# Linear attention times a SwiGLU gate on one core: a seventh stored key operand, and the last two stores on SyncE

## The chip, the core and the metric

The kernel runs on one core of one Trainium2 chip. It uses that core's engines: TensorE (PE, matrix products; its weight loads are listed as PEld), VectorE (DVE), ScalarE (ACT), GpSimd (POOL) and SyncE (SP). SyncE only issues DMAs here. GpSimd issues DMAs and does some elementwise work. Sixteen DMA engines move the data of both. The metric is device time in microseconds (us) of one execution; less is better.

## The reference

x has 2048 rows of 1024 columns. The result is x + s * g, with

```python
def _A_ref(x, wqkv, wo):                 # 32 heads of width 32
    q, k, v = ...                        # x @ wqkv, by head
    phi = lambda t: jnp.where(t > 0, t + 1, jnp.exp(t)) + 1e-6
    pq, pk = phi(q), phi(k)
    kv = jnp.einsum("bhsd,bhse->bhde", pk, v)
    z = jnp.einsum("bhsd->bhd", pk)
    num = jnp.einsum("bhqd,bhde->bhqe", pq, kv)
    den = jnp.einsum("bhqd,bhd->bhq", pq, z)[..., None] + 1e-6
    return (num / den) @ wo              # heads side by side again

def _B_ref(x, w1, w3, w2):
    return (_silu(x @ w1) * (x @ w3)) @ w2

xn = _layernorm(x)
s = _A_ref(xn, A_wqkv, A_wo)
g = _silu(_B_ref(xn, B_w1, B_w3, B_w2))
return x + s * g
```

All inputs and the result are float32.

## The kernel before

**Products.** Every large product is made of blocks by a scheme with seven products in place of eight; the sums of blocks that it needs are operands of their own (names such as A11, S1 to S4 on the left, B11, T1 to T4 on the right). Each operand is split into a high and a low part (`split`, L91: a cast on ScalarE, L95, and a subtraction on VectorE, L96), and each block product is three matmuls (`mm3`, L100).

**Stages.** The rows are taken in two halves (h = 0, 1). In each half the keys and queries are made, and later the gate and up products of the SwiGLU layer. Between the queries and the gate of the second half stand the row products: since kv = pk^T v and v = xn w_v, the kernel first forms pk^T xn (over all 2048 rows) and multiplies by w_v afterwards. Then follow the attention's output products and the second layer (w2), whose last pass finishes the result.

**Key sums (`key_rows`, L519).** For each half and each of four pairs, four blocks of keys pass through phi, are turned by TensorE (L513) and written out by GpSimd as operands of the row products (`keep_keys`, L516): Y00, Y01, Y10, and the sums R5, R2 and R4. Six operands of 256 KB are stored for each of the eight pairs. y00 and r2 are tiles from `small`, which has six buffers (tag "c") shared with the products' results c22, c21, c12 and others.

**Row products (`row_products`, L558).** Seven products (`ROWS`, L625) go over four steps each: h = 0, 1 and t = 0, 2, so 28 steps. A step loads two row tiles of the left operand (x_d, L572) and two of the right one (y_d, L570) into one tile `xy<i>_<h><t>` of tag "raw", which has two buffers; splits them into tiles of tag "b", which has eight, four to a step; and multiplies each of the two row tiles into four banks. A step is 24 matmuls. The load for a step is written two steps ahead. The seventh product needs R2 - Y00: its steps load Y00 into a further tile `yy` (tag "job", four buffers) and subtract it on GpSimd (L583) before the split.

```python
            if less:
                other = job_tile([P, 2, C], f"yy{i}_{h}{t}")
                rows(other, less)
        ...
            if other is not None:
                nc.gpsimd.tensor_sub(out=raw[:, 2:], in0=raw[:, 2:], in1=other)
```

**Work between.** During the row products, small pieces of other work run between the steps: the denominators (L857 on TensorE, one for each of sixteen loads `pqd` into "job" tiles, then `r` and its store r_d). After them comes the division of the queries (`divide`, L872): each piece `qd<m>_<k>` is a "job" tile filled by two loads from r_d (L882) and two from pq_d (L884) on SyncE. In the last steps the weights of the first gate product (`wg`, L326) are loaded into a "raw" tile.

**Order.** The program is written in one stream. A scheduler places each instruction in its engine's queue by a modelled time and by when a buffer comes free; each queue is then worked through in order, and an instruction that has to wait holds all behind it. SyncE's queue is one: a load that waits for its tile holds every later load.

**The end (`finish`, L1191).** Each of the four blocks (t, n) of a 256-row tile m is finished by a silu on ScalarE (L1198), a product with s (`ss`, loaded on SyncE) and an addition of x (`xs`) on VectorE (L1199, L1201), and a store on GpSimd (L1202). The last tile is m = 7; its blocks end in the order (1,1), (0,0), (1,0), (0,1).

Of the kernel before, what the change touches and what calls it, by code (L numbers as in the profile page):

```python
# [16 lines left out]
P = 128  # L17
C = 512
# [4 lines left out]
def tile_linear_attention_times_swiglu(  # L23
# [58 lines left out]
    s_d = [dram.tile([P, D], F32, name=f"s_d{t}") for t in range(S // P)]  # L82
    AOPS = ["A11", "S2", "S3", "S1", "A12", "A22", "S4"]
    XS = ["A11", "A12", "S1", "S3", "A22", "S2", "S4"]
    YS = ["Y00", "Y01", "Y10", "R5", "R2", "R4"]
    x_d = [dram.tile([P, TH // 2, len(XS), C], F32, name=f"x_d{h}") for h in range(NH)]
    y_d = [dram.tile([P, TH // 2, len(YS), ND // 2, P], F32, name=f"y_d{h}") for h in range(NH)]
    g_d = [dram.tile([P, ND // 2, C], F32, name=f"g_d{n}") for n in range(4)]
# [27 lines left out]
    def small(name):  # L116
        return pc.tile([P, C], F32, tag="c", name=name)
# [401 lines left out]
    def key_rows(h, pair):  # L519

        rows = {}

        def use(n, c, src):
            j = 2 * pair + n
            pk = signed(f"pk{h}_{j}_{c}")
            z = st.tile([P, 1], F32, tag="z", name="z")
            phi(src, pk, z)
            nc.vector.scalar_tensor_tensor(zacc[:, j:j + 1], z, C * 1e-6, zacc[:, j:j + 1],
                                           op0=ALU.add, op1=ALU.add)
            later.append([3, lambda: turn(n, c, pk)])  # L530

        def turn(n, c, pk):
            V = nc.vector
            p_ = turned(pk, f"k{h}_{pair}_{n}{c}")
            if (c, n) == (0, 0):
                y00 = small(f"y00_{h}_{pair}")
                nc.scalar.activation(y00, p_, AF.Identity, bias=eps)  # L537
                keep_keys(h, pair, "Y00", y00)
            elif (c, n) == (1, 1):
                rows["y01"] = job_tile([P, 2, C], f"y01_{h}_{pair}")  # L540
                nc.scalar.copy(out=rows["y01"][:, 1], in_=p_)
            elif (c, n) == (1, 0):
                y10, r5 = (rows.setdefault("y10", job_tile([P, 2, C], f"y10_{h}_{pair}"))[:, e] for e in range(2))
                nc.scalar.activation(y10, p_, AF.Identity, bias=eps)
                V.tensor_sub(out=r5, in0=rows["y01"][:, 1], in1=p_)
                keep_keys(h, pair, "Y10", y10)
                keep_keys(h, pair, "R5", r5)
            else:
                (y01, r4), r5, r2 = (rows["y01"][:, e] for e in range(2)), rows["y10"][:, 1], small(f"r2_{h}_{pair}")
                nc.scalar.activation(y01, p_, AF.Identity, bias=eps)  # L550
                V.scalar_tensor_tensor(r4, p_, 2e-6, r4, op0=ALU.add, op1=ALU.add)
                V.scalar_tensor_tensor(r2, p_, 1e-6, r5, op0=ALU.add, op1=ALU.add)
                for n_, t in (("Y01", y01), ("R4", r4), ("R2", r2)):
                    keep_keys(h, pair, n_, t)

        return use

    def row_products():  # L558

        nonlocal stages  # L560
        ks = [(h, t) for h in range(NH) for t in range(0, TH // 2, 2)]
        steps = [(i, *k) for i in range(len(ROWS)) for k in ks]

        def load(i, h, t):
            x_, y_, less = ROWS[i]
            raw = praw.tile([P, 4, C], F32, tag="raw", name=f"xy{i}_{h}{t}")

            def rows(dst, n):
                src = y_d[h][:, t:t + 2, YS.index(n)].rearrange("p t j d -> p t (j d)")
                nc.sync.dma_start(out=dst, in_=src)  # L570

            nc.sync.dma_start(out=raw[:, :2], in_=x_d[h][:, t:t + 2, XS.index(x_)])  # L572
            rows(raw[:, 2:], y_)
            other = None
            if less:
                other = job_tile([P, 2, C], f"yy{i}_{h}{t}")
                rows(other, less)
            return raw, other

        def ready(i, h, t):  # L580
            raw, other = data[i, h, t]
            if other is not None:
                nc.gpsimd.tensor_sub(out=raw[:, 2:], in0=raw[:, 2:], in1=other)  # L583
            out = []
            for e in range(2):
                pair = []
                for n in range(2):
                    o = pb.tile([P, 2, C], FR, tag="b", name=f"xy{n}_{i}_{h}{t + e}")
                    split(o, raw[:, 2 * n + e])
                    pair.append(o)  # L590
                out.append(pair)
            return out

        data = {s: load(*s) for s in steps[:2]}
        split_ = {steps[0]: ready(*steps[0])}
        u, v, b = {}, {}, {}
        M = range(ND // 2)
        for at, s in enumerate(steps):
            i, h, t = s
            if at + 2 < len(steps):  # L600
                data[steps[at + 2]] = load(*steps[at + 2])
            if at + 1 < len(steps):
                split_[steps[at + 1]] = ready(*steps[at + 1])
            if at + 2 == len(steps):
                ops["g1_0_"].ask()
                stages = in_turn(groups[after_rows:])
            if at + 1 == len(steps):
                for _ in range(3):
                    next(stages)
            begins, ends = s[1:] == ks[0], s[1:] == ks[-1]  # L610
            onto = i in (1, 5)
            if begins and not onto:
                b = {m: bank(f"g{i}_{m}") for m in M}
            for e, (x_, y_) in enumerate(split_.pop(s)):
                for m in M:
                    c = slice(m * P, (m + 1) * P)
                    last = mm3(b[m], (x_[:, 0, c], x_[:, 1, c]), (y_[:, 0], y_[:, 1]),
                               begins and e == 0 and not onto, ends and e == 1)
                    if ends and e == 1:
                        row_sums(i, m, b[m], u, v)  # L620
                catch_up(last)
                yield
            del data[s]

    ROWS = [("A22", "Y10", None), ("A12", "Y00", None), ("S2", "R2", None), ("S1", "R4", None),  # L625
            ("S3", "R5", None), ("S4", "Y01", None), ("A11", "R2", "Y00")]

    def row_sums(i, m, b, u, v):
        V = nc.vector
# [558 lines left out]
    def added_by_dma(m, t):  # L1188
        return m < ADDED and t == 1

    def finish(m, t, n, a):  # L1191
        r0, cols = (2 * m + t) * P, slice(n * C, (n + 1) * C)
        ss = small(f"ss{m}_{t}{n}")
        nc.sync.dma_start(out=ss, in_=s_d[2 * m + t][:, cols])
        if not added_by_dma(m, t):
            xs = small(f"xs{m}_{t}{n}")
            nc.sync.dma_start(out=xs, in_=x[r0:r0 + P, cols])
        nc.scalar.activation(a, a, AF.Silu)  # L1198
        nc.vector.tensor_mul(a, a, ss)  # L1199
        if not added_by_dma(m, t):  # L1200
            nc.vector.tensor_add(a, a, xs)  # L1201
            nc.gpsimd.dma_start(out=out[r0:r0 + P, cols], in_=a)  # L1202
        else:
            nc.gpsimd.dma_start(out=out[r0:r0 + P, cols], in_=a, accum_op=ALU.add)

# [96 lines left out]
```

## Time and profile before

| | us |
|---|---|
| median of 3 runs | 2360.43 |
| lowest and highest of these runs | 2357.89, 2363.99 |
| the profiled execution, its own time | 2364.7 |
| span of the profiled execution | 2362.9 |
| granted TensorE clock, mean | 0.992 of full |

The span goes from the first to the last instruction that the profiler recorded, and the execution's own time lies a little around it. In the rows below, a row of the timeline is: start, duration, engine, line, operation, output <- inputs, count, and in brackets the idle time before it and what ended it. A row of the view of waits is: total us, times, longest. A row of the chain of waits is: start, duration, what. "SPq" and "POOLq" are instructions of a queue itself, such as an issued DMA or a drain. In rows of a tile or a line, three times stand for shortest, median and longest in ns, then the first and the last start.

### The profile page before, as it was taken

How to read it: one execution, taken by the hardware profiler on the slowest of the kernel's cores; microseconds unless marked ns; L12 is line 12 of the kernel's file. 1: busy time of each engine (PE TensorE's matmuls, PEld its weight loads, DVE VectorE, ACT ScalarE, POOL GpSimd, SP SyncE). 2: the span in 40 equal slices, each digit the busy share in tenths (PEclk: the TensorE clock that was granted, in tenths of full speed). 3: DMA queues.
4: the chain of work that ended last, by engine and by line, in shares of the span. 5: the costliest groups of instructions: out<-in, count | busy, mean ns of one | idle time of the engine just before them, and what ended most of it. 6: DMA issues, size and time to landing. Idle time of an engine off the chain costs nothing.

```text
span 2362.9 us, 30966 instructions
## 1 busy us (share of the span) xinstructions
PE 2306.2 (98%) x10368; PEld 1893.2 (80%) x10368; DVE 1775.7 (75%) x2822; ACT 924.5 (39%) x1639; POOL 697.2 (30%) x852
## 2 busy tenths in 40 slices
PE   6999999999999999998999999999999999999998
PEld 5788878888887888776888888888887788888876
DVE  8887888898877775656867688887745666767798
ACT  5555343423232555433233332334324534342433
POOL 5120433377866111012423435342310000000033
PEclk9999999999999999999999999999999999999999
DMA  6555455576669546776665567665756565766688
GB/s 236 165 174 178 156 179 183 172 228 220 225 210 321 196 134 205 255 257 207 201 193 181 188 200 218 195 216 168 230 153 195 181 198 172 225 208 182 191 265 260
DMA packets 354015, 479.69 MB, mean 203 GB/s; under 512 B 24144, under 2 KB 262736, under 8 KB 353744
## 3 DMA queue, kind: packets, MB, share of 16 engines
q1 hardware_dynamic: 316608, 359.20, 48.1%
q0 software_dynamic: 37248, 118.52, 15.2%
q8 instruction: 81, 1.33, 0.2%
q14 instruction: 78, 0.64, 0.1%
HBM read 308.81 MB, written 172.49 MB: 204 GB/s over the span
## 4 chain that ended last, share of the span: by engine, by line
PE 74%; DMA 5%; DVE 5%; issue 2%; ACT 1%; SPq 1%; POOL 0%; DVEq 0%; POOLq 0%; ACTq 0%
PE g L103 2%; PE g L104 2%; PE g L105 2%; PE cB L103 1%; PE cB L104 1%; PE cB L105 1%; PE dB L103 1%; PE dB L104 1%; PE dB L105 1%; PE aB L105 1%; PE aB L103 1%; PE aB L104 1%; DMA rA12B<-h_d 1%; PE bB L105 1%; PE bB L103 1%
## 5 line engine op out<-in xcount | busy, mean ns | idle before, releaser
L756 POOL DMA_DIRECT2D h_d<-sg x112 | 82.7, 739 | 262.5 <-DVE sg L752 183.9
L1069 POOL DMA_DIRECT2D u_d<-uB x32 | 17.3, 541 | 407.9 <-DVE uB L1052 354.8
L96 DVE TENSOR_TENSOR xy<-xy,xy 128x512 fp32r<-128x512 f32 x112 | 75.0, 704 | 70.4 <-ACT xy L95 70.2
L95 ACT CAST xy<-xy 128x512 fp32r<-128x512 f32 x112 | 65.1, 620 | 109.3 <-PE g L105 62.5
L103 PE MATMUL g<-xy,xy 128*128 128x512 f32 x224 | 82.3, 403 | 7.1 <-ACT xy L95 7.1
L104 PE MATMUL g<-xy,xy 128*128 128x512 f32 x224 | 88.5, 395 | 0.0
L105 PE MATMUL g<-xy,xy 128*128 128x512 f32 x224 | 87.9, 393 | 0.0
L517 POOL DMA_DIRECT2D y_d<-y x40 | 28.6, 718 | 141.9 <-ACT y L537 81.6
L1052 DVE TENSOR_TENSOR acc<-cB,acc 128x512 f32<-128x512 f32 x50 | 34.4, 688 | 40.2 <-PE cB L105 40.2
L1052 DVE TENSOR_TENSOR acc<-dB,acc 128x512 f32<-128x512 f32 x56 | 38.5, 688 | 31.0 <-PE dB L105 30.8
L736 POOL TENSOR_TENSOR hs<-hs,sg 128x256 f32<-128x256 f32 x56 | 61.1, 1090 | 0.1
L103 PEld LDWEIGHTS g<-xy,xy 128*128 128x128 f32 x224 | 42.1, 190 | 21.9 <-ACT xy L95 9.6
L738 POOL TENSOR_TENSOR hs<-sg 128x256 f32<-128x256 f32 x56 | 57.7, 1031 | 0.0
L894 POOL DMA_DIRECT2D qs_d<-qd x32 | 18.0, 564 | 119.3 <-DVE qd L890 82.0
L1183 POOL DMA_DIRECT2D s_d<-s x32 | 17.3, 541 | 117.7 <-DVE s L1052 70.9
L735 POOL TENSOR_TENSOR hs<-sg,sg 128x256 f32<-128x256 f32 x56 | 50.8, 906 | 1.2
L104 PEld LDWEIGHTS g<-xy,xy 128*128 128x128 f32 x224 | 42.7, 190 | 9.9 <-issue 0.8
L739 POOL TENSOR_TENSOR hs<-sg,hs 128x256 f32<-128x256 f32 x56 | 49.9, 892 | 1.5
L105 PEld LDWEIGHTS g<-xy,xy 128*128 128x128 f32 x224 | 42.6, 190 | 9.2
L771 POOL TENSOR_TENSOR w<-w 128x256 f32<-128x256 f32 x28 | 28.2, 1006 | 70.9 <-DMA w<-in_B_w 69.7
L764 POOL DMA_DIRECT2D h_d<-hs x60 | 45.8, 765 | 4.3 <-POOL hs L739 2.4
L674 POOL DMA_DIRECT2D pq_d<-pq x32 | 17.5, 546 | 91.1 <-DVE pq L507 88.3
(5315 smaller groups left out, 8330.1 us busy)
## 6 DMA issues: line engine op xcount, KB each, us to landing
h_d<-hs POOLq DMA_DIRECT2D x60, 256.0 KB, 3.5
h_d<-sg POOLq DMA_DIRECT2D x56, 256.0 KB, 3.9
w<-in_B_w SPq DMA_DIRECT2D x56, 256.0 KB
wt_d<-w SPq DMA_DIRECT2D x28, 512.0 KB
xy<-x_d SPq DMA_DIRECT2D x28, 512.0 KB
xy<-y_d SPq DMA_DIRECT2D x28, 512.0 KB
h_d<-hs SPq DMA_DIRECT2D x52, 256.0 KB
qs_d<-qd POOLq DMA_DIRECT2D x32, 384.0 KB, 3.9
```

The source lines that it names most:

```text
L95: nc.scalar.copy(out=hi, in_=src)
L96: return nc.vector.tensor_sub(out=lo, in0=src, in1=hi.bitcast(F32))
L103: nc.tensor.matmul(acc, lhsT=wh, rhs=ah, start=start, stop=False, skip_group_check=True)
L104: nc.tensor.matmul(acc, lhsT=wh, rhs=al, start=False, stop=False, skip_group_check=True)
L105: return nc.tensor.matmul(acc, lhsT=wl, rhs=ah, start=False, stop=stop, skip_group_check=True)
L735: e.tensor_add(out=s1, in0=a21, in1=a22)
L736: e.tensor_sub(out=s2, in0=s1, in1=a11)
L738: e.tensor_sub(out=s3, in0=a11, in1=a21)
L739: e.tensor_sub(out=s4, in0=a12, in1=s2)
L756: nc.gpsimd.dma_start(out=h_d[i][2 * h + c][:, 2 * n:4 * n + 2, k], in_=src)
L764: queue.dma_start(out=h_d[i][2 * h + c][:, 6 + 4 * e:10 + 4 * e, k], in_=o[e].rearrange("p (e s) -> p e s", s=P))
L1052: return V.tensor_add(out=c, in0=src, in1=c)
```

## The change

The difference R2 - Y00 is made with the other key sums, in Y00's tile, and is stored as a seventh operand R6; the row products load R6 where they loaded R2 and Y00. At the end, the loads of ss and xs become a function `fetch`, called for block (0,1) of the last tile before the work of block (1,0), and the stores of these two blocks are issued on SyncE.

```diff
-    YS = ["Y00", "Y01", "Y10", "R5", "R2", "R4"]
+    YS = ["Y00", "Y01", "Y10", "R5", "R2", "R4", "R6"]
...
             if (c, n) == (0, 0):
-                y00 = small(f"y00_{h}_{pair}")
+                y00 = rows["y00"] = small(f"y00_{h}_{pair}")
                 nc.scalar.activation(y00, p_, AF.Identity, bias=eps)
                 keep_keys(h, pair, "Y00", y00)
...
                 for n_, t in (("Y01", y01), ("R4", r4), ("R2", r2)):
                     keep_keys(h, pair, n_, t)
+                V.tensor_sub(out=rows["y00"], in0=r2, in1=rows["y00"])
+                keep_keys(h, pair, "R6", rows["y00"])
...
-            x_, y_, less = ROWS[i]
+            x_, y_ = ROWS[i]
...
-            other = None
-            if less:
-                other = job_tile([P, 2, C], f"yy{i}_{h}{t}")
-                rows(other, less)
-            return raw, other
+            return raw
 
         def ready(i, h, t):
-            raw, other = data[i, h, t]
-            if other is not None:
-                nc.gpsimd.tensor_sub(out=raw[:, 2:], in0=raw[:, 2:], in1=other)
-            out = []
+            raw, out = data[i, h, t], []
...
-    ROWS = [("A22", "Y10", None), ("A12", "Y00", None), ("S2", "R2", None), ("S1", "R4", None),
-            ("S3", "R5", None), ("S4", "Y01", None), ("A11", "R2", "Y00")]
+    ROWS = [("A22", "Y10"), ("A12", "Y00"), ("S2", "R2"), ("S1", "R4"), ("S3", "R5"), ("S4", "Y01"), ("A11", "R6")]
...
-    def finish(m, t, n, a):
+    factors = {}
+
+    def fetch(m, t, n):
         r0, cols = (2 * m + t) * P, slice(n * C, (n + 1) * C)
-        ss = small(f"ss{m}_{t}{n}")
+        ss, xs = small(f"ss{m}_{t}{n}"), None
         nc.sync.dma_start(out=ss, in_=s_d[2 * m + t][:, cols])
         if not added_by_dma(m, t):
             xs = small(f"xs{m}_{t}{n}")
             nc.sync.dma_start(out=xs, in_=x[r0:r0 + P, cols])
+        factors[m, t, n] = ss, xs
+
+    def finish(m, t, n, a):
+        r0, cols = (2 * m + t) * P, slice(n * C, (n + 1) * C)
+        if (m, t, n) not in factors:
+            fetch(m, t, n)
+        if (m, t, n) == (NG - 1, 1, 0):
+            fetch(m, 0, 1)
+        ss, xs = factors[m, t, n]
+        queue = nc.sync if m == NG - 1 and t != n else nc.gpsimd
         nc.scalar.activation(a, a, AF.Silu)
         nc.vector.tensor_mul(a, a, ss)
         if not added_by_dma(m, t):
             nc.vector.tensor_add(a, a, xs)
-            nc.gpsimd.dma_start(out=out[r0:r0 + P, cols], in_=a)
+            queue.dma_start(out=out[r0:r0 + P, cols], in_=a)
```

**How instructions move.** The first place is SyncE's queue in the last steps of the row products. xy6_10 and xy6_12 are the tiles of the last two steps (seventh product, second half), yy6 the tiles of Y00, qd0_k the pieces of the division for the first 256 rows. Before:

```order
L570 DMA yy6_10_8913<-y_d1_167 128x2x512
L570 DMA yy6_12_8967<-y_d1_167 128x2x512
L572 DMA xy6_10_8910<-x_d1_165 128x2x512
L570 DMA xy6_10_8910<-y_d1_167 128x2x512
L882 DMA qd0_0_9113<-r_d0_136 128x1x256
L884 DMA qd0_0_9113<-pq_d0_0_79 128x256
L882 DMA qd0_0_9113<-r_d0_136 128x1x256
L884 DMA qd0_0_9113<-pq_d1_0_83 128x256
L882 DMA qd0_1_9118<-r_d0_136 128x1x256
L884 DMA qd0_1_9118<-pq_d0_0_79 128x256
L882 DMA qd0_1_9118<-r_d0_136 128x1x256
L572 DMA xy6_12_8964<-x_d1_165 128x2x512
```

In the changed kernel, ending with the first load of wg (whose tile comes from "raw"):

```order
L878 DMA qd0_2_9127<-pq_d1_0_83 128x256
L574 DMA xy6_10_8921<-x_d1_165 128x2x512
L572 DMA xy6_10_8921<-y_d1_167 128x2x512
L876 DMA qd0_3_9194<-r_d0_136 128x1x256
L878 DMA qd0_3_9194<-pq_d0_0_79 128x256
L876 DMA qd0_3_9194<-r_d0_136 128x1x256
L574 DMA xy6_12_8972<-x_d1_165 128x2x512
L572 DMA xy6_12_8972<-y_d1_167 128x2x512
L878 DMA qd0_3_9194<-pq_d1_0_83 128x256
L326 DMA wg1_0__9023<-in_B_w1 128x8x256
```

The yy loads are gone, and the qd loads stand where a "job" tile comes free: qd0_0 to qd0_2 are now ahead of the rows shown, and three of qd0_3's four loads stand between the last two steps' loads, where seven of qd0_0 and qd0_1 stood. wg, which stood behind eight further qd loads, now has one of qd0_3 between it and the last step's.

The second place is VectorE's queue at the first key pair's last sums (first half). Before:

```order
L551 SCALAR_TENSOR_TENSOR y01_0_0_952<-trk0_0_10_1039,y01_0_0_952 128x512
L552 SCALAR_TENSOR_TENSOR r2_0_0_1044<-trk0_0_10_1039,y10_0_0_989 128x512
L470 TENSOR_TENSOR c22k0_2__1063<-ck0_2__1020,uk0_2__388 128x512
L96 TENSOR_TENSOR B22k0_3__1065<-wk0_3__974,B22k0_3__1065 128x512
L476 TENSOR_TENSOR c22k0_2__1063<-dk0_2__1021,c22k0_2__1063 128x512
```

In the changed kernel:

```order
L551 SCALAR_TENSOR_TENSOR y01_0_0_952<-trk0_0_10_1039,y01_0_0_952 128x512
L552 SCALAR_TENSOR_TENSOR r2_0_0_1044<-trk0_0_10_1039,y10_0_0_989 128x512
L470 TENSOR_TENSOR c22k0_2__1065<-ck0_2__1020,uk0_2__388 128x512
L555 TENSOR_TENSOR y00_0_0_807<-r2_0_0_1044,y00_0_0_807 128x512
L96 TENSOR_TENSOR B22k0_3__1067<-wk0_3__974,B22k0_3__1067 128x512
L476 TENSOR_TENSOR c22k0_2__1065<-dk0_2__1021,c22k0_2__1065 128x512
```

The new subtraction stands one instruction behind r2, ahead of a split and of the addition that waits for TensorE. GpSimd's queue gets the store of the same tile right behind r2's store.

The third place is the end. GpSimd's queue before, with the four stores of the last tile:

```order
L1065 TENSOR_TENSOR acc7_15075<-acc7_15075,uB4_7_19805 128x512
L1202 DMA out_0<-acc6_15074 128x512
L1202 DMA out_0<-acc7_15075 128x512 x4
L1298 UNCONDITIONAL_BRANCH
L1298 ISA
```

SyncE's queue in the changed kernel:

```order
L1190 DMA ss7_10_20031<-s_d15_163 128x512
L1193 DMA xs7_10_20033<-in_A_x 128x512
L1190 DMA ss7_01_20035<-s_d14_162 128x512
L1193 DMA xs7_01_20037<-in_A_x 128x512
L1208 DMA out_0<-acc7_15079 128x512 x2
L1304 UNCONDITIONAL_BRANCH
```

GpSimd keeps two of the four stores, and the other two are the last DMAs on SyncE, behind the four loads, whose order is as before.

## The prediction

> **What bounds the kernel now.** I read the page's busy times first, then who TensorE waited for, then the timeline of TensorE around the longest of these waits, then the chain of waits behind it, and last the final ten microseconds.
>
> ```profile
> span 2362.9 us, 30966 instructions
> PE 2306.2 (98%) x10368; PEld 1893.2 (80%) x10368; DVE 1775.7 (75%) x2822; ACT 924.5 (39%) x1639; POOL 697.2 (30%) x852
> ```
>
> TensorE is busy for 2306.2 of 2362.9 us. So nothing is gained except in the 57 us in which it is not busy, and in matmuls that run slowly. In the stretch from 900 to 1100 us, where the row products end, the view of waits has two rows for TensorE, and its timeline shows both:
>
> ```profile
> PE g L103 <- ACT xy L95: 7.1, 2, 6.9
> PE bg__9128 L103 <- ACT T2g__9056 L95: 1.0, 1, 1.0
> 1078.41 0.39 PE L105 MATMUL g<-xy,xy 128*128 128x512 f32 x1
> 1085.66 2.07 PE L103 MATMUL g<-xy,xy 128*128 128x512 f32 x4 [6.87 <-ACT xy L95]
> 1093.48 0.39 PE L103 MATMUL ag__9096<-A,B11g__9047 128*128 128x512 f32 x1
> 1095.98 0.39 PE L105 MATMUL ag__9096<-A,B11g__9047 128*128 128x512 f32 x1
> 1097.40 0.50 PE L103 MATMUL bg__9128<-S,T2g__9056 128*128 128x512 f32 x1 [1.03 <-ACT T2g__9056 L95]
> 1085.60:1088.00 2.40, 2.34 (x6) 1.85 (x7) 1.90 (x3) 1.05 (x3) 0.00 (x0) 0.50 0.49 149
> ```
>
> The twelve matmuls of ag start from 1093.48 to 1095.98, so one follows another every 0.227 us. The last step of the row products (24 matmuls: two row tiles, four banks, three products) should take 24 x 0.227 = 5.45 us. It begins where the step before ends, 1078.41 + 0.23 = 1078.64, and ag starts at 1093.48: 14.84 us. So the stall costs 9.4 us, not 6.9: the last row (busy times by window; the 0.50 is the granted clock) shows that the step then runs at half clock. Behind it bg waits another 1097.40 - 1096.21 = 1.2 us. What held the step is read from the timelines of GpSimd and SyncE and from the chain of waits:
>
> ```profile
> 1069.95 2.39 POOL L583 TENSOR_TENSOR xy<-xy,yy 128x1024 f32<-128x1024 f32 x1 [3.45 <-DMA xy<-y_d]
> 1082.63 2.33 POOL L583 TENSOR_TENSOR xy<-xy,yy 128x1024 f32<-128x1024 f32 x1 [8.67 <-DMA xy<-y_d]
> 1063.70 0.46 SPq L570 DMA_DIRECT2D xy<-y_d  x1
> 1071.29 1.08 SPq L572 DMA_DIRECT2D xy<-x_d  x1
> 1072.40 1.07 SPq L570 DMA_DIRECT2D xy<-y_d  x1
> 1067.34 3.25 SPq L884
> 1070.63 9.28 DMA qd<-r_d
> 1079.98 10.15 DMA wg__9019<-in_B_w
> ```
>
> The last pair of operands is asked for at 1071.29 and 1072.40, lands until 1082.63, is subtracted on GpSimd for 2.33 us, and is then split on ScalarE and VectorE. The request was late because seven loads of qd stand ahead of it in SyncE's queue, one of which took 3.25 us to issue.
>
> The other place is the end of the program:
>
> ```profile
> 2352.94 0.54 POOL L1202 DMA_DIRECT2D out<-acc  x1 [1.23 <-DVE acc L1201]
> 2356.13 1.14 POOL L1202 DMA_DIRECT2D out<-acc  x2 [2.65 <-DVE acc L1201]
> 2355.15 1.29 DVE L1201 TENSOR_TENSOR acc<-acc,xs 128x512 f32<-128x512 f32 x2
> L1298 POOLq DRAIN x3: 45/93/5453, 2356.7 to 2362.7; - x3
> L1298 SPq DRAIN x3: 7/7/13, 2359.8 to 2362.4; - x3
> out<-acc POOLq DMA_DIRECT2D x2, 256.0 KB, 2.4
> ```
>
> VectorE ends at 2356.44. SyncE has seen every store land, and drains, from 2359.8. But GpSimd's drain, begun with its last store at 2356.7, runs for 5.45 us, to 2362.15, and 0.75 us later the span ends. So the end waits 2.3 us for GpSimd alone.
>
> **Part 1: the subtraction leaves the row products.** Removed are four loads of yy and four subtractions; their tiles go to qd, whose loads move forward in SyncE's queue.
>
> ```profile
> L570 SPq DMA_DIRECT2D yy<-y_d x4: 359/360/360, 1037.3 to 1058.1; - x4
> L95 ACT CAST xy<-xy 128x512 fp32r<-128x512 f32 x112 | 65.1, 620 | 109.3 <-PE g L105 62.5
> L96 DVE TENSOR_TENSOR xy<-xy,xy 128x512 fp32r<-128x512 f32 x112 | 75.0, 704 | 70.4 <-ACT xy L95 70.2
> 1064.46 0.64 PE L857 MATMUL den<-pqd,zb 128*32 128x256 f32 x8
> 1067.45 0.67 DVE L96 TENSOR_TENSOR xy<-xy,xy 128x512 fp32r<-128x512 f32 x1
> L882 SPq DMA_DIRECT2D qd<-r_d x64: 523/530/2544, 1064.3 to 1574.1; - x64
> L884 SPq DMA_DIRECT2D qd<-pq_d x64: 432/477/3247, 1065.0 to 1574.7; - x64
> ```
>
> In the new order the last pair stands behind three loads of qd0_3 instead of seven of qd0_0 and qd0_1. The first of the three needs the tile that the last denominator reads, so it waits for that matmul: 1064.46 + 0.64 = 1065.1. Three issues at 0.53, 0.48 and 0.53 us, with a gap between, bring the x load to about 1066.8. Its tile is the one that the step two earlier split; its last split ended at 1067.45 + 0.67 = 1068.1 even with the subtraction before it. So the y load goes out between 1067.2 and 1068.5, four to five us sooner than 1072.40. Its landing I bound by its two neighbours: 1069.95 - 1063.70 = 6.25 us and 1082.63 - 1072.40 = 10.23 us. It lands between 1073.5 and 1078.7, and with one cast (0.62) and one split (0.69) the step may start between 1074.8 and 1080.0. TensorE is there at 1078.64. The stall that remains is 0 to 1.4 us; I take 0.4, nearer the lower end, since the 2 MB of yy no longer pass ahead of this load. Gain 9.0.
>
> The load of wg waits for a tile that is freed by the splits of the third step. Before, it was issued at 1079.98, behind qd loads; now only one qd load stands between it and the last pair, so it leaves at about 1070 and, at its old 10.15 us, lands at 1080.2. TensorE needs B11g at 1078.64 + 0.4 + 5.45 = 1084.5, after 1.3 us of splitting: covered with 3 us to spare. wg had landed at 1079.98 + 10.15 = 1090.13, and bg started 7.3 us after that, which now gives 1087.5; ag ends at 1084.5 + 2.7 = 1087.2. So most of bg's 1.2 us goes: between 0 and 1.2, I take 0.8. Part 1: **9.8 us**, bounds 2.4 (only the subtraction saved) and 10.8 (all).
>
> **Part 2: the eighth part of the key sums.** Each of the eight pairs gets one more subtraction on VectorE and one more store on GpSimd, 256 KB.
>
> ```profile
> 60.00:150.00 90.00, 84.98 (x394) 69.71 (x395) 74.21 (x141) 49.51 (x86) 18.80 (x27) 0.96 0.52 165
> 800.00:900.00 100.00, 100.00 (x462) 82.58 (x461) 76.15 (x137) 55.79 (x95) 17.11 (x26) 1.00 0.41 132
> 107.05 0.69 DVE L476 TENSOR_TENSOR c22k__1063<-dk__1021,c22k__1063 128x512 f32<-128x512 f32 x1 [1.87 <-PE dk__1021 L105]
> 104.14 0.82 POOL L517 DMA_DIRECT2D y_d<-r  x1
> 110.72 0.68 DVE L491 TENSOR_TENSOR c21k__1124<-ck__1020,uk__388 128x512 f32<-128x512 f32 x1
> DMA to landing us min/median/max: 2.7/3.0/6.6
> ```
>
> On VectorE that is 8 x 0.69 = 5.5 us (a subtraction of this shape takes as long as L476's 0.69). In the windows of both key stages (columns: TensorE, weight loads, VectorE, ScalarE, GpSimd) VectorE is busy 74 of 90 and 76 of 100 us, and the first new subtraction falls into the 1.87 us in which VectorE waits for TensorE before 107.05. With that cover gone it would cost 5.5 at most; nothing is removed here, so no gain. I take 0: TensorE is busy 100.00 of 100 us in the second stage, so nothing that VectorE does there is late for it. GpSimd is busy 19 of 90. The new store reads the tile of Y00, so four of the six tiles of tag "c" are held longer. Next to be late would be c21k at 110.72, which now takes the tile of R2: R2's store was issued at 104.14, and with the longest landing of these stores, 6.6, it is free at 110.74, with the median 3.0 at 107.1. Hidden.
>
> **Part 3: the two last stores.** They are issued on SyncE, where nothing is behind them, at 2355.84 and 2356.44 when VectorE ends each, instead of 2356.13 and 2356.73.
>
> ```profile
> 2350.87 0.33 SPq L1197 DMA_DIRECT2D xs<-in_A_x  x1
> 2318.30 4.30 DMA ss<-s_d
> ```
>
> GpSimd's last store is then the one at 2352.94; its drain begins at 2353.48 and at the same 5.45 us ends at 2358.9, ahead of SyncE. SyncE's end: no store of this kind leaves SyncE in this trace at rest, so its landing is bounded by GpSimd's 2.4 us (then everything is 0.3 us earlier: SyncE drains at 2359.55) and by a load's 4.30 us, taken under full traffic (2356.44 + 4.30 + 0.8 = 2361.5). The end comes 0.75 later, at 2360.3 or 2362.25: a gain between 0.65 and 2.6. I take **2.3**, near the first, since the queues are empty then.
>
> The row has GpSimd's drain 2.3 us behind SyncE's. The Trainium skill, "DMA: Bandwidth & Descriptors", Issuing engines are not separate DMA queues, speaks against this part: all DMAs run on the same engines, and another issuer saves only the sequencer's time. By it the sum would hold 0.3 here instead of 2.3; this is the second rival.
>
> **Sum.** 9.8 + 0 + 2.3 = 12.1 us. The profiled execution took 2364.7 us around a span of 2362.9 and would take 2352.6; the runs shown have a median of 2360.43, 4.3 us below it, so I predict 2360.43 - 12.1 = **2348.3 us**.
>
> **Rivals.**
> 1. The last pair is hardly earlier, because transfers and not the queue set its landing. For it: it took 10.23 us where its neighbour took 6.25. Against it: four loads of 512 KB fewer ahead of it. Then only the 2.4 us of subtraction and the end are won: 4.7, time 2355.7.
> 2. The end waits for something other than GpSimd's drain: 9.8 + 0.3, time 2350.3. For it: a drain of 5.45 us behind a store that lands in 2.4 is odd, and may be counted from elsewhere. Against it: SyncE stands ready 2.3 us before.
> 3. The subtractions in the key stages are not covered: 12.1 - 5.5 = 6.6, time 2353.8. For it: VectorE is busy 82% of the first stage. Against it: the gap of 1.87 us where the first one goes, and a TensorE that never waits in the second stage.
> 4. Slower: SyncE's queue. Sixteen qd loads in pieces of 1 KB now stand between the operands' loads. If those of qd0_2 and qd0_3 (eight) each issue as slowly as the slowest seen, 3.25 and 2.54, they hold the queue for 4 x 5.8 = 23 us instead of 4 x 1.0, so the last y load leaves 19 us after 1067.2, at 1086.3; the step starts at 1086.3 + 10.23 + 1.3 = 1097.8 instead of 1085.66. That is +12.1, less 2.3 at the end: 2370.2. It turns slower from a y load issued after about 1077. For it: one issue of 3.25 us. Against it: the medians, 0.53 and 0.48.
>
> **How the numbers follow.** Forecast 0.60, rival 1 0.15, rival 2 0.13, rival 3 0.06, rival 4 0.06. The runs shown lie between 2357.89 and 2363.99, so I add 2.5 us of scatter. All bounds at their best give 10.8 + 2.6 = 13.4, 2347.0, less scatter 2344; the range reaches up over rivals 2, 3 and most of 1 to 2357, and leaves out rival 4: 2343.5 to 2357. Faster by over 0.3% (about what a measurement of this kernel can tell from no change; below 2353.3): nearly all of the forecast and of rival 2, a third of rivals 1 and 3, 0.75. Slower by over 0.3%: rival 4, 0.06. Within: 0.19.
>
> **What would show it.** Right: no wait over 1 us at L103 for xy, the granted clock at 1.0 through the row products, the last x load issued near 1067, wg before 1072; no wait of TensorE in the key stages; GpSimd's last drain ended before SyncE's, and the span ending under 4.2 us after VectorE instead of 6.5. Wrong: a wait at the last step that outlives the subtraction, SyncE's qd issues of several us, VectorE waiting on a store in the key stages, or GpSimd's drain still last.

## The result and the profile after

| | before | changed |
|---|---|---|
| median of 6 runs each, us | 2364.52 | 2347.99 |
| lowest to highest, us | 2357.89 to 2368.56 | 2345.70 to 2350.73 |
| ratio, with its 95% interval | | 0.9933 (0.9916 to 0.9951) |
| span of the profiled execution, us | 2362.9 | 2348.1 |

The ratio is 15.8 us, 11.6 to 19.9; the two profiled spans lie 14.8 us apart. The forecast was 12.1 us, 2348.3 us. The rows follow the order of those of the kernel before. Busy times of the changed kernel:

```profile
span 2348.1 us, 30976 instructions
PE 2300.6 (98%) x10368; PEld 1890.5 (81%) x10368; DVE 1780.3 (76%) x2830; ACT 924.7 (39%) x1639; POOL 689.8 (29%) x854
```

TensorE is busy for 5.6 us less with as many matmuls: matmuls that ran at half clock run at full clock. The whole list of TensorE's waits from 900 to 1100 us, and the busy times by window around the end of the row products, of the changed kernel (columns: start and end of the window, its length, then busy us and, in brackets, instructions of TensorE, weight loads, VectorE, ScalarE, GpSimd, then granted clock, share of the DMA engines, GB/s):

```profile
PE g L104 <- DVE xy L96: 0.2, 1, 0.2
1070.00:1110.00 40.00, 39.78 (x174) 32.20 (x173) 31.12 (x55) 17.07 (x29) 4.93 (x8) 1.00 0.53 177
```

The same window of the kernel before:

```profile
1070.00:1110.00 40.00, 31.87 (x128) 25.16 (x127) 25.25 (x39) 13.65 (x23) 8.78 (x9) 0.91 0.65 202
```

The wait of 6.9 us for the split operands and the one of 1.0 us for bg are gone, the clock is 1.00, and 46 matmuls more stand in the same 40 us. The timeline of SyncE and the chain of waits show why:

```profile
1060.43 0.53 SPq L876 DMA_DIRECT2D qd<-r_d  x1
1061.01 0.60 SPq L878 DMA_DIRECT2D qd<-pq_d  x1
1061.66 0.53 SPq L876 DMA_DIRECT2D qd<-r_d  x1
1062.29 1.34 SPq L574 DMA_DIRECT2D xy<-x_d  x1
1063.67 0.59 SPq L572 DMA_DIRECT2D xy<-y_d  x1
1064.31 0.55 SPq L878 DMA_DIRECT2D qd<-pq_d  x1
1070.23 0.38 SPq L326 DMA_DIRECT2D wg__9023<-in_B_w  x1
1063.67 9.39 DMA xy<-y_d
```

The last pair goes out at 1062.29 and 1063.67 behind three loads of qd, as the order had it; TensorE is 4.7 us earlier here than before, so these are 1067.0 and 1068.4 by the clock of the kernel before. The y load lands in 9.39 us, the cast and split follow, and the step starts almost without a stop. wg leaves at 1070.23 (1075.1 by the clock of the kernel before), and its first cast starts at 1077.0.

The end, in the timelines of VectorE, SyncE and GpSimd, and the drains of both queues (the shortest, median and longest duration in ns, then the first and the last start; the long drain of GpSimd is the first to start):

```profile
2341.21 1.29 DVE L1207 TENSOR_TENSOR acc<-acc,xs 128x512 f32<-128x512 f32 x2
2341.92 0.94 SPq L1208 DMA_DIRECT2D out<-acc  x2
2338.99 0.54 POOL L1208 DMA_DIRECT2D out<-acc  x1 [1.24 <-DVE acc L1207]
L1304 POOLq DRAIN  x3: 45/102/8312, 2339.0 to 2347.8; - x3
L1304 SPq DRAIN  x3: 7/7/13, 2345.0 to 2347.5; - x3
```

VectorE ends at 2342.50, SyncE stands ready at 2345.1, and GpSimd's drain, begun with its last store at 2339.0, takes 8.31 us instead of 5.45 and ends at 2347.3. The span ends 5.6 us after VectorE, where 6.5 stood before and 4.2 was forecast (6.5 - 2.3). The drain still sets the end.

### The profile page after: what moved, and what is told of

The parts are those of the page before. It is cut to its first block, busy times and chain, and to the rows that moved or that the text cites. A ratio compares the mean times of both kernels' runs of the same rounds, so it can differ in the third digit from the quotient of the medians.

```text
span 2348.1 us, 30976 instructions
## 1 busy us (share of the span) xinstructions
PE 2300.6 (98%) x10368; PEld 1890.5 (81%) x10368; DVE 1780.3 (76%) x2830; ACT 924.7 (39%) x1639; POOL 689.8 (29%) x854
## 4 chain that ended last, share of the span: by engine, by line
PE 73%; issue 5%; DVE 4%; DMA 3%; ACT 1%; POOL 0%; SPq 0%; DVEq 0%; POOLq 0%; ACTq 0%
PE g L103 2%; PE g L104 2%; PE g L105 2%; PE dB L104 1%; PE dB L105 1%; PE dB L103 1%; PE aB L103 1%; PE cB L103 1%; PE cB L104 1%; PE aB L104 1%; PE aB L105 1%; PE cB L105 1%; PE bB L105 1%; PE bB L104 1%; PE bB L103 1%
## 5 line engine op out<-in xcount | busy, mean ns | idle before, releaser
L517 POOL DMA_DIRECT2D y_d<-y x48 | 34.6, 721 | 140.0 <-ACT y L537 79.9
L103 PEld LDWEIGHTS g<-xy,xy 128*128 128x128 f32 x224 | 41.8, 188 | 14.2 <-issue 4.5
L95 ACT CAST XS4B<-rS4B 128x384 fp32r<-128x384 f32 (+1 forms) x40 | 19.7, 493 | 60.7 <-PE cB L105 41.1
```

What stands on the lines that cost most here:

```text
L95: nc.scalar.copy(out=hi, in_=src)
L103: nc.tensor.matmul(acc, lhsT=wh, rhs=ah, start=start, stop=False, skip_group_check=True)
```

## The experiments

Twelve more kernels ran, two of them the kernel before and the changed kernel once more. To place what each saves, the table cuts every profiled execution at the same four places in TensorE's order of matmuls, counted from the first (the starts of the matmuls there were read from the traces; in the kernel before the cuts lie at 282, 809, 1018 and 1103 us), and at the last one. The six columns on the right are the us from one cut to the next, the last one from the last matmul's start to the end of the span. A ratio is that of the runs of the kernel to those of the kernel before on the same chip; before_again and r6_half are one run each and have none.

| kernel | ratio (95%) | 0 to 282 | to 809 | to 1018 | to 1103 (row products' end) | to the last matmul | end |
|---|---|---|---|---|---|---|---|
| before | | 282.3 | 527.1 | 208.2 | 84.9 | 1249.5 | 10.9 |
| before_again | | 283.6 | 527.4 | 208.2 | 84.7 | 1251.0 | 10.8 |
| changed | 0.9933 (0.9916 to 0.9951) | 282.7 | 522.3 | 208.2 | 74.6 | 1250.3 | 9.9 |
| after_again | 0.9935 (0.9921 to 0.9949) | 283.6 | 521.1 | 208.2 | 74.6 | 1247.2 | 9.8 |
| r6_only | 0.9953 (0.9941 to 0.9966) | 281.4 | 522.3 | 208.2 | 74.1 | 1249.0 | 14.6 |
| tail_only | 0.9988 (0.9980 to 0.9997) | 283.8 | 527.8 | 208.2 | 85.7 | 1249.1 | 7.6 |
| keys_only | 0.9995 (0.9986 to 1.0004) | 283.5 | 522.5 | 208.2 | 86.9 | 1249.3 | 14.2 |
| queue_only | 0.9988 (0.9979 to 0.9997) | 282.8 | 524.5 | 208.2 | 83.1 | 1249.7 | 10.8 |
| queue_wg | 0.9949 (0.9936 to 0.9962) | 283.6 | 528.2 | 208.2 | 74.0 | 1250.9 | 11.1 |
| loads_kept | 0.9968 (0.9956 to 0.9981) | 282.6 | 521.8 | 208.2 | 82.1 | 1249.6 | 10.0 |
| r6_sync | 0.9921 (0.9908 to 0.9935) | 281.3 | 520.2 | 208.2 | 74.5 | 1247.8 | 8.4 |
| last_four_sync | 0.9922 (0.9908 to 0.9936) | 281.6 | 524.5 | 208.2 | 73.7 | 1250.4 | 7.8 |
| r6_half (one run) | | 282.9 | 520.4 | 208.2 | 74.5 | 1245.3 | 8.7 |
| queue_and_tail | 0.9919 (0.9905 to 0.9932) | 282.0 | 525.2 | 208.2 | 73.9 | 1249.8 | 7.9 |

The columns show at a glance where the changed kernel wins: 10.3 us at the row products' end, and, not forecast, about 5 us between 282 and 809 us. Two executions of one kernel differ by 0.9 and 1.3 us in the first column, by 0.3 and 1.2 in the second and by 1.5 and 3.1 in the fifth, so differences of that size between kernels say nothing there.

### The two halves of the change, and its parts

**r6_only**: the changed kernel with `finish` as before, all stores of the result on GpSimd.

```diff
-        queue = nc.sync if m == NG - 1 and t != n else nc.gpsimd
-            queue.dma_start(out=out[r0:r0 + P, cols], in_=a)
+            nc.gpsimd.dma_start(out=out[r0:r0 + P, cols], in_=a)
```

> The change without its end: R6 is made, stored and loaded, the last stores stay on GpSimd. By the prediction's sum 9.8 us are saved (ratio 0.9958), the span ends 6.5 us after VectorE as before, no TensorE wait for xy over 1 us, and the last x load of the row products is asked for near 1062 to 1067. If the changed kernel's time came from the end or from the granted clock instead, the ratio stays above 0.998. If the half-clock windows near 300 and 760 us that the kernel before shows (and the changed one does not) are set by this part, none is seen here; if they are chance of one execution, they may be back.

Measured: 0.9953, 11.1 us (8.0 to 14.0), with 10.8 us at the row products and the clock at 1.00 there. No half clock shows near 302 and 757 us. But the span ends 9.5 us after VectorE, where the 6.5 of before were expected.

**tail_only**: the kernel before with the changed `fetch` and `finish`, and nothing else.

> Kernel before with only the end changed. By the prediction 2.3 us are saved and GpSimd's drain ends ahead of SyncE's. By what the changed kernel shows (GpSimd's drain 8.3 us, ending 2.2 us after SyncE's in both) only 0.9 us are saved, GpSimd's drain lasts some 8 us and again ends 2.2 us after SyncE's. Row products as before: a wait of 6.9 us for xy. If the half-clock windows near 300 and 760 us belong to the order of the kernel before, they are here too.

Measured: 0.9988, 2.8 us (0.7 to 4.7); the span ends 3.1 us after VectorE. GpSimd's drain and SyncE's:

```profile
L1310 POOLq DRAIN  x3: 45/93/5290, 2355.7 to 2362.0; - x3
L1310 SPq DRAIN  x3: 7/7/13, 2361.5 to 2361.8; - x3
```

It ends at 2361.0, before SyncE's drain at 2361.5. So it does not follow SyncE by 2.2 us; the rival formed after the result has fallen.

**keys_only**: the kernel before with R6 made and stored, and not used.

```diff
+                V.tensor_sub(out=rows["y00"], in0=r2, in1=rows["y00"])
+                keep_keys(h, pair, "R6", rows["y00"])
```

> Kernel before, with R6 also made and stored but not used: the row products still load R2 and Y00 and subtract. By the prediction the eight subtractions and stores cost 0 (ratio 1.000, within 0.001); by its third rival 5.5 us (ratio 1.0023). The wait of 6.9 us at the last step of the row products stays, since seven loads of qd still stand ahead of the last pair.

Measured: 0.9995 (0.9986 to 1.0004), no difference, as forecast. The table says that this nothing is a sum: in the profiled execution 4.6 us are won between 282 and 809 us, 2.0 us are lost at the row products' end, where TensorE waits for xy for 8.4 us in all instead of 7.1 and for gc for 0.8, and 3.3 us are lost at the end, where the drain is 3.02 us longer than before. Whether R6 is the cause of the 2.0 us was not tried. The drain:

```profile
L1300 POOLq DRAIN  x3: 45/102/8475, 2355.3 to 2364.3; - x3
```

The win is in two places, near 302 and 757 us. TensorE's waits over the whole span, and the window around the first place, of keys_only:

```profile
PE bk__6499 L103 <- ACT T2k__6350 L95: 1.5, 1, 1.5
PE cg__2665 L103 <- DVE c22g__2697 L470: 1.1, 1, 1.1
299.00:307.00 8.00, 6.92 (x31) 5.40 (x30) 6.15 (x11) 3.17 (x7) 2.01 (x3) 1.00 0.56 173
```

The same of the kernel before:

```profile
PE bk__6491 L103 <- ACT T2k__6342 L95: 2.2, 1, 2.2
PE cg__2657 L103 <- DVE c22g__2689 L470: 2.1, 1, 2.1
299.00:307.00 8.00, 5.88 (x20) 4.39 (x19) 5.98 (x9) 2.77 (x6) 1.88 (x3) 0.79 0.56 170
```

Both waits are shorter, and behind the first the clock stays at 1.00 where it was 0.79. Over the 14 traces: in the six without R6 the wait near 302 us is 2.1 to 2.2 us, and five of them then show half clock; in the eight with R6 it is 1.0 to 1.4 us, and none does. Near 757 us the wait is 0.7 to 1.5 us in six of the eight, but 2.0 and 2.5 us in r6_only and last_four_sync; without R6 it is 1.9 to 2.5 us in five of the six and 1.4 in queue_and_tail. So at the first place the shorter wait goes with R6 in every trace, and at the second in most. At both places together, 11 of 13 waits of 1.9 us or more were followed by half clock, and none of 15 waits of 1.5 us or less. The Trainium skill, "TensorE: Matmul & The Clock Gate", Why this matters for your kernels, warns of gaps over some 3 us between bursts of matmuls; here waits of 1.9 to 2.5 us were enough.

**queue_only**: the kernel before; only the loads of qd are placed behind the last pair's y load in SyncE's queue (`asked[-1]` is the y load asked for last).

```diff
+            with tc.issue_after(asked[-1].ins):
                 for e in range(2):
...
                     nc.sync.dma_start(out=t[:, e], in_=pq_d[j // JG][c][:, j % JG, cols])
```

> Kernel before, with the loads of qd placed behind the last pair of operands in SyncE's queue; subtraction, its loads and the end stay. If SyncE's queue set the stall (prediction), the last y load goes out within 2 us after its tile is free (by 1069), and of the stall of 9.4 us 2 to 4 are left (the subtraction of 2.33 us and a landing of up to 10 us): ratio 0.997. If transfers set the landing (first rival), the last y load still lands after 1080, and the stall stays over 7 us: ratio 1.000. wg stands behind nine loads of qd, so bg may wait longer than the 1.0 us of before.

Measured: 0.9988, 2.8 us (0.7 to 5.0). TensorE's waits from 900 to 1110 us, and the two issues that matter in SyncE's timeline:

```profile
PE ag__9096 L103 <- ACT B11g__9047 L95: 4.0, 1, 4.0
PE g L103 <- ACT xy L95: 1.6, 2, 0.8
PE bg__9128 L103 <- ACT T2g__9056 L95: 1.5, 1, 1.5
1067.02 0.50 SPq L570 DMA_DIRECT2D xy<-y_d  x1
1075.88 0.60 SPq L326 DMA_DIRECT2D wg__9019<-in_B_w  x1
```

The wait for the pair falls from 7.1 to 1.6 us with the subtraction still in its path. But nine loads of qd now stand ahead of wg, and its first operand takes over the wait: the row products' end takes 83.1 us, hardly less than 84.9. The stall was handed on to the next load in the queue.

**queue_wg**: the same, with the loads of qd also behind the first load of wg.

```diff
                 ops["g1_0_"].ask()
+                asked.append(fetched[0])
```

> Kernel before, with the loads of qd behind the last pair of operands and behind the first load of wg in SyncE's queue; the subtraction, the loads of Y00, the key sums and the end are those of before. If SyncE's queue made the stall and its half clock (the kernel with qd behind the last pair alone kept 1.6 us of waiting for xy but then waited 4.0 us for wg's first operand), both waits are now under 2 us and 7 to 9 us of the row products' 10.3 are won: ratio 0.9962 to 0.997. If the subtraction itself was needed for it, at most 3 us are won: ratio 0.9988 or more. Rival: the later division holds the attention's work, and a new wait shows after 1100 us.

Measured: 0.9949, 12.1 us (9.0 to 15.1). The row products' end takes 74.0 us, 10.9 less than before where 7 to 9 were expected, and about as long as in the changed kernel, and no wait of TensorE is left between 900 and 1110 us; the subtraction and the loads of Y00 are all there. SyncE's timeline, and GpSimd's row of the last subtraction, which starts when the y load has landed:

```profile
1070.58 0.36 SPq L572 DMA_DIRECT2D xy<-x_d  x1
1070.99 0.63 SPq L570 DMA_DIRECT2D xy<-y_d  x1
1077.21 0.37 SPq L326 DMA_DIRECT2D wg__9019<-in_B_w  x1
1077.67 0.66 SPq L884 DMA_DIRECT2D qd<-r_d  x1
1077.45 2.54 POOL L583 TENSOR_TENSOR xy<-xy,yy 128x1024 f32<-128x1024 f32 x1 [1.29 <-DMA xy<-y_d]
```

The new order helps in two ways of about equal size. The step before ends at 1080.85 here and at 1078.64 in the kernel before; counted back from there, the y load is asked for 3.6 us sooner. And it lands in 6.46 us (1070.99 to 1077.45) instead of 10.23. No load of qd is issued beside it here, in the kernel before eight are issued between 1066.7 and 1078.1; that this is why it lands faster is likely, and was not tried by itself.

No later wait came in its place: the stretch to the last matmul is 1250.9 us, beside 1249.5 and 1251.0 of the kernel before. So the division was not late for being asked for last.

**loads_kept**: the changed kernel, with the four loads of Y00 put back into tiles that nothing reads.

```diff
             rows(raw[:, 2:], y_)
+            if i == 6:
+                rows(job_tile([P, 2, C], f"yy{i}_{h}{t}"), "Y00")
```

> Changed kernel, with the four loads of Y00 into further tiles put back, unread; nothing is subtracted. If only the queue's order matters, the last pair is asked for by 1065, no wait for xy over 1 us, and the ratio is that of the changed kernel, 0.9935. If the 2 MB of Y00 had filled the transfers (first rival of the prediction), the last y load takes its old 10 us, lands after 1073, and a wait of 1 to 5 us for xy is back: ratio 0.994 to 0.996.

Measured: 0.9968, a wait of 6.0 us again, but one step earlier than expected. SyncE's timeline, with the first and the last of the nine loads of qd between the pairs:

```profile
1052.89 0.47 SPq L880 DMA_DIRECT2D qd<-pq_d  x1
1059.73 1.31 SPq L880 DMA_DIRECT2D qd<-pq_d  x1
1061.14 0.37 SPq L574 DMA_DIRECT2D xy<-x_d  x1
1061.94 1.73 SPq L572 DMA_DIRECT2D xy<-y_d  x1
```

The added loads also moved the loads of qd: nine of them now stand in front of the pair of the last step but one, which left at 1055.72 in the changed kernel and leaves at 1061.14 here. So this kernel does not tell the transfers of Y00 from the order, as it was meant to; queue_wg does, since it moves the same 2 MB and has no stall.

**before_again**: the kernel before, profiled once more.

> The kernel before, profiled again. If its half-clock windows near 300 and 760 us belong to its waits there (2.1 us for c22g, 2.2 for T2k), at least one is seen again; the row products show the wait of 6.9 us and GpSimd's last drain 5.45 us.

Measured: 2367.53 us in one run; waits of 6.9, 2.1 and 2.0 us at the three places, half clock behind each, and the drain:

```profile
L1298 POOLq DRAIN  x3: 45/102/5453, 2359.5 to 2365.5; - x3
```

### What sets the end

**r6_sync**: the changed kernel, R6's stores on SyncE.

```diff
-                keep_keys(h, pair, "R6", rows["y00"])
+                nc.sync.dma_start(out=y_d[h][:, :, YS.index("R6"), pair], in_=rows["y00"].rearrange("p (t d) -> p t d", d=P))
```

> Changed kernel with R6's eight stores on SyncE instead of GpSimd. Theory: GpSimd's last drain grows with what GpSimd has stored (5.45 and 5.29 us without R6's stores, 8.48 and 8.31 us with them). Then the drain is 5.3 us here, ends ahead of SyncE's, the span ends 3.1 us after VectorE instead of 5.6, and some 2.5 us are saved against the changed kernel (ratio to before near 0.992). Rival: the drain is long because of the earlier end of the other engines or the new order, not of the stores; then it stays near 8.3 us and nothing is saved. Against both: a store that waits for VectorE in SyncE's queue could hold loads in the key stages.

**last_four_sync**: the changed kernel, all four stores of the last tile on SyncE.

```diff
-        queue = nc.sync if m == NG - 1 and t != n else nc.gpsimd
+        queue = nc.sync if m == NG - 1 else nc.gpsimd
```

> Changed kernel with all four stores of the last tile on SyncE. Theory (the drain is counted from GpSimd's last DMA and lasts 8.1 to 8.3 us): it starts with the last store of the tile before, near 2331, ends near 2339, ahead of SyncE, and the span ends 3.1 us after VectorE: 2.5 us less than the changed kernel. Rival (the drain waits for SyncE's end, 2.2 us behind it as in the kernels before and after): it lasts over 14 us and the span ends 5.6 us after VectorE.

**after_again**: the changed kernel once more.

> The changed kernel once more. Ratio 0.993 as before; if its freedom from half-clock windows near 300 and 760 us belongs to its order, none is seen here either; if it was chance, one may show. TensorE's wait of 3.1 us for acc at 2290 us is gone if it was chance. GpSimd's drain again 8.3 us.

**r6_half**: as r6_sync, but the second half's four stores of R6 stay on GpSimd.

> Changed kernel with R6's four stores of the first half on SyncE and the four of the second on GpSimd. If GpSimd's drain grows with each of its stores of 512 pieces (3.02 us for eight), it is 5.29 + 1.5 = 6.8 us. If it is a step (a count that passes a limit), it is 5.3 or 8.3 us.

GpSimd's and SyncE's drains, of r6_sync, of r6_half, of last_four_sync and of after_again:

```profile
L1304 POOLq DRAIN  x3: 45/93/5290, 2333.7 to 2340.3; - x3
L1304 SPq DRAIN  x3: 7/7/13, 2339.7 to 2340.0; - x3
```

```profile
L1304 POOLq DRAIN  x3: 45/102/6678, 2332.6 to 2339.8; - x3
```

```profile
L1304 POOLq DRAIN  x3: 45/102/9320, 2333.4 to 2345.9; - x3
L1304 SPq DRAIN  x3: 7/7/13, 2345.3 to 2345.6; - x3
```

```profile
L1304 POOLq DRAIN  x3: 45/93/8312, 2335.5 to 2344.3; - x3
```

The length repeats to the nanosecond in after_again, and follows R6's stores on GpSimd: 5.29 us with none, 6.68 with four, 8.31 with eight. It is not the changed order, since r6_sync has that order and 5.29 us. In last_four_sync the drain starts at 2333.4 (its last store had to wait until 2334.2) and ends at 2342.7, 2.7 us ahead of SyncE: again GpSimd does not wait for SyncE. In both kernels the span now ends 3.2 to 3.3 us after VectorE, set by SyncE, against 5.6 in the changed kernel. In the runs of the same comparison r6_sync's median is 1.6 us and last_four_sync's 1.1 us below after_again's; the intervals overlap, so that they are faster is likely by the profile and not shown by the clock.

In after_again neither place at 302 and 757 us shows half clock, and the wait of 3.1 us for acc near 2290 us, which the first profile of the changed kernel had, is gone: it comes and goes between executions.

### A kernel without R6

**queue_and_tail**: queue_wg and tail_only together.

> Kernel before with two things only: the loads of qd behind the last pair and behind wg in SyncE's queue, and the changed end. No R6: its stores are not made, Y00 is loaded and subtracted in the row products as before. If the changed kernel's gain is SyncE's order and the end, the two add up: 0.9949 and 0.9988 give 0.9937, the changed kernel's ratio. GpSimd's last drain is 5.3 us and ends ahead of SyncE's, the span ends 3.1 us after VectorE, no wait for xy over 2 us. If R6 itself is worth more (the waits near 300 and 760 us), the ratio stays above 0.995.

Measured: 0.9919 (0.9905 to 0.9932), not slower than the changed kernel (0.9933 and 0.9935; the intervals overlap), without its seventh operand. The row products' end takes 73.9 us, and the span ends 3.1 us after VectorE. Two numbers were missed. The ratio lies below the 0.9937 that the two parts give; in the profile the wait near 757 us is 1.4 us and no half clock follows it, where queue_wg and tail_only waited 2.5 us and had one step of it. And the drain is 6.20 us with as many stores on GpSimd as tail_only and r6_sync have, where it took 5.29:

```profile
L1312 POOLq DRAIN  x3: 45/102/6197, 2340.1 to 2346.8; - x3
```

## Why the prediction came out right, step by step

**Part 1 held, by its mechanism and its size.** 9.8 us were forecast, 10.3 measured at the row products' end in both profiles of the changed kernel. The last step and its stall took 14.84 us and now take 6.15 (from 1073.73 to ag at 1079.88), so 8.7 of the 9.0 forecast; bg gave 1.1 where 0.8 was taken; another 0.5 us came from the steps before. Counted back from the end of the step before, the last y load is asked for 3.8 us sooner (10.06 us ahead, 6.24 before), lands 0.8 us faster, and its first matmul follows 2.3 us sooner, without the subtraction: together the 6.9 us of the wait. The prediction had these terms: a request four to five us sooner, and 2.4 us for the subtraction. The landing, 9.39 us, was near the upper bound (10.23) and not the lower, so that the 2 MB of Y00 no longer pass made little difference, and the stall that remains is 0.7 us and not 0.4. The upper bound of 10.8 for this part is 0.2 more than its terms, 9.4 and 1.2.

The load of wg came out in time by luck. The prediction had it leave at about 1070, land in 10.15 us and be ready 3 us early. By the clock of the kernel before it left at 1075.1, five us later, but it landed in 6.8 us at most, and its first operand was split 1.6 us before TensorE needed it (1078.3 and 1079.88).

What the prediction did not see is that neither the subtraction nor the loads of Y00 had to go: queue_wg keeps both and has the whole gain, by the order of SyncE's queue alone. In the change that order came as a by-product: without the tiles of Y00 the scheduler found room for the loads of qd earlier.

**Part 2 was near 0 by luck: two effects that it left out have opposite signs.** In the key stages the cost was indeed covered: TensorE's busy time from 60 to 150 us is 0.4 us less in the changed kernel, and up to 282 us it is 0.4 us later, less than two executions of one kernel differ; the ratio of keys_only is 0.9995. But the eight stores make GpSimd's last drain 3.0 us longer, at the other end of the program, and with R6 a wait of TensorE near 302 us is always shorter and one near 757 us mostly, so that its clock stays up: over all traces the stretch from 282 to 809 us takes 521.9 us in the mean of the eight traces with R6 and 526.7 in the six without, 4.8 us less. Why the waits are shorter is open: VectorE's order at 302 us is the same, and TensorE comes later in some of these kernels and earlier in others.

**Part 3 failed at one sentence**: that the drain "at the same 5.45 us ends at 2358.9, ahead of SyncE". It is the right forecast for tail_only (3.3 us less at the end in the profile, 2.8 us in the runs, 2.3 forecast, where SyncE stood ready 2.3 us after VectorE, sooner than the 3.1 of the better bound), and the wrong one for the change as a whole, whose own stores lengthen the drain to 8.31 us: it kept 0.9 us of the 2.3. GpSimd's last drain still ends behind SyncE's, and the span ends 5.6 us after VectorE, which the prediction named as the sign of a wrong step.

**The sum.** Forecast 9.8 + 0 + 2.3 = 12.1. In the two profiles of the table: -0.4 up to 282 us, +4.8 to 809, +10.3 at the row products, -0.8 to the last matmul, +1.0 at the end, together 14.8 by the spans. So 12.1 came true as a sum of terms of which only the row products' came out at its size, and the stretch from 282 to 809 us, which was not in it, made up for the end. That the forecast median was met to 0.3 us is luck besides: 15.8 us were saved, and the three runs of the kernel before that it started from lay 4 us lower than the six of the comparison.

**The rivals.** The first (the last pair is hardly earlier, because transfers set its landing) is refuted as it stood: the pair is asked for 3.8 us sooner, and queue_wg has no stall with the 2 MB of Y00 still passing. But the landing has a share in the stall too: in queue_wg, with no load of qd beside it, the y load lands in 6.46 us instead of 10.23. The second (the end waits for something other than GpSimd's drain) named the right place: the end does wait for the drain, but the doubt behind it was just, since the drain's length is set elsewhere. In the change as a whole 0.9 us came at the end, nearer to its 0.3 than to 2.3. By the Trainium skill's rule that the prediction weighed, "DMA: Bandwidth & Descriptors", Issuing engines are not separate DMA queues, tail_only would have saved 0.3 us. It saved 3.3 in its profile (3.4 counted from VectorE's end): 2.3 because GpSimd's drain may begin 3.5 us before VectorE ends, and 1.1 because SyncE stands ready 2.3 us after VectorE instead of 3.5. The measurement decides: the issuer mattered here. The third (VectorE not covered) did not show. The fourth (SyncE blocked by the small pieces) did not occur in the changed kernel, but loads_kept shows its mechanism: nine loads of qd in front of a pair cost 6.0 us of waiting.

## What to carry to other kernels

A stall at a load is often the stall of its queue: list what stands ahead of the late load and why each of those has to wait, and move that, before removing work from the load's own path. Then look at the load behind it, which inherits the delay. Stores that are free where they are issued can still be paid for at the end of the program, so read the last instructions of every queue before and after a change.

## What was not expected of the hardware

The drain that ends GpSimd's queue starts with its last DMA and grows with DMAs issued long before: eight more stores of 256 KB, each in 512 pieces by its tile's shape, made it 3.02 us longer (5.45 to 8.48 and 5.29 to 8.31), two stores of 128 pieces fewer made it 0.16 us shorter (5.45 to 5.29). It was 5.453 and 8.312 us in both profiles of the kernel before and of the changed kernel, and within 4 ns of that in most kernels with the same stores, but 6.20 us in queue_and_tail where 5.29 was due, and 8.48 us from the last store in last_four_sync, where two stores fewer than 8.31 would give 8.15. What it counts was not tried further.

In the clock's own record half clock came in steps of 3.41 us, and at the two places near 302 and 757 us one or two of them followed a wait of 1.9 us or more in 11 of 13 cases. One step at half clock loses 1.7 us, nearly as much again as the wait. Taken over the whole stretch from 70 to 2330 us of all 14 traces, it is not the length of a single wait that counts. Every change of the clock lies on a grid of 3.41 us, which begins at a different time in each execution, and half clock goes with the idle time of TensorE in one slot of that grid. Counted in the gaps of over 0.45 us between the starts of matmuls, less 0.23 us for the matmul itself, and in slots at full clock, all 18 slots with 2.1 us or more idle were followed by half clock, 4 of 11 with 1.8 to 2.1 us, and none with less. Two slots of the kernel before, and two of the changed kernel's first profile:

```profile
298.55:301.96 3.41, 1.40 (x7) 0.81 (x5) 3.38 (x6) 2.16 (x4) 2.33 (x3) 1.00 0.74 225
301.96:305.37 3.41, 3.31 (x8) 2.63 (x9) 3.05 (x6) 0.63 (x1) 0.00 (x0) 0.50 0.61 188
2289.17:2292.58 3.41, 1.56 (x7) 0.94 (x6) 3.41 (x6) 1.77 (x4) 1.50 (x1) 1.00 0.99 330
2292.58:2296.00 3.42, 2.18 (x10) 1.81 (x11) 3.42 (x7) 0.51 (x1) 1.45 (x2) 1.00 0.81 219
```

The wait of 2.1 us near 302 us lies almost wholly in one slot, and the next slot runs at half clock. The wait of 3.1 us near 2290 us is longer, but falls into two slots, 2.06 us of it into the first, and the clock stays. Near 1810 us two waits of 1.1 to 1.5 us in one slot brought half clock in three executions (before_again, queue_only, queue_wg). So whether a wait costs clock also depends on where the grid lies, which no run here controls.
